# A newly written order for attention and a mixer on one core: other loads wait, and small tiles stand in 58 stretches for 52

## The chip, the core and the metric

The kernel runs on one core of a Trainium2 chip. The metric is the device time of one execution in microseconds (us); the time before is the median of three runs. The engines are TensorE (PE in the profile; its weight loads are PEld), VectorE (DVE), ScalarE (ACT), GpSimd (POOL) and SyncE (SP). Loads from memory are issued by GpSimd; stores and transposing transfers by SyncE.

## What is computed

Eight batches of 12 heads, 448 tokens, head size 64, then a mixer over tokens and channels on the 768 joined columns:

```python
scores = scale * np.matmul(q, k.transpose(0, 1, 3, 2))
attn = np.maximum(scores, 0.0) ** 2 / S
x = np.matmul(attn, v)                      # heads side by side: (8, 448, 768)
h = np.maximum(xt @ w_tok1, 0.0) @ w_tok2   # xt: x with tokens last; 448 -> 256 -> 448
u = x + h.transpose(0, 2, 1)
h2 = np.maximum(u @ w_ch1, 0.0) @ w_ch2     # 768 -> 1536 -> 768
out = u + h2
```

The inputs are float32, the products are made in bfloat16.

## The kernel before

The attention is done in 24 groups of four heads, three groups to a batch. The program first makes a list of named operations with what each depends on, and then emits them in the order of a table, `ORDER` (line 73), a text of some two thousand words. A word is a name, and behind the colon the PSUM banks of a product (`S0.4:75`), the engine of an evacuation (`:A` ScalarE, `:D` VectorE), or the gate of a load. Each engine takes its own words in the order of the table, so the table fixes five queues and, by their place, what waits behind what. `Order.run` (line 51) reads it. The names that matter here:

- `ldk9.0`, `ldq..`, `ldv..`: loads of half a group's keys, queries or values, cast on the way (line 371, GpSimd). `ldf` brings the first queries through SyncE and ScalarE, and `cast` turns them to bfloat16. `wt`, `wc1.i` and `wc2.i` load the weights of the two mixers (lines 382, 389, 397, 406); `wc1.i` covers four of the twelve column blocks `e` of the first channel product, and the second product needs all three `wc2.i`.
- `ident` makes the identity matrix on GpSimd. `T s` transposes keys and queries of groups 0 to 9 on TensorE against it (line 472), `cp` copies the result out of PSUM. From group 10 on `ik`/`iq` rearrange them and `xk`/`xq` transpose them by a transfer of SyncE's queue (line 497).
- `S s.c`: one block of scores, four products of 64 x 64 tiles (line 515), a quartet; `r` takes the positive part out of PSUM, `q` squares it, `V s.c` multiplies by the values (line 542, also a quartet), `xe` evacuates.
- `xd s` transposes the group's result by a transfer of SyncE's queue (line 566; for groups 0 to 5 TensorE does it, `X`, line 579, with the copy `xc`), `t1` and `t2` are the token mixer (lines 588 and 597) with `rt` between, `u` adds (line 601), `ub` transposes u by a transfer (line 610).
- `C1` (line 623) or, from batch 2 on, `M1` with its sums `tu`, `s1`, `d1`, `y1` (line 780) is the first channel product; `C2` (line 713) and `M2` with `h`, `d2` (line 847) the second. `M1` and `M2` make seven products of eight by sums of blocks, `w1` and `w2` are such sums of the weights. `st` stores 64 rows of the result (line 668).
- `fill:b*n` puts products without use on TensorE (line 967): n quarters of a product of 512 columns, whole ones first and the rest of 128.

A gate makes a load wait on GpSimd's queue until the named transfer of SyncE has landed:

```python
            if o.eng == 'POOL' and how:
                self.behind(o.ins, self.ops[how].ins)
```

Every load also waits for the one eight places before it, and SyncE's transfers do the same among themselves, since each of the two queues has eight semaphores; all loads land in the order of their issue. On TensorE a product of 64 x 64 tiles (`T`, `S`, `V`) and one of 128 rows (all others) follow each other in stretches of a kind; the table before has 52 stretches of small tiles.

## Time and profile before

| what | value |
|---|---|
| median of three runs | 344.29 us (342.73 to 345.22) |
| the profiled execution | 346.45 us, span 344.4 us |
| granted TensorE clock | 1.000 |
| TensorE, VectorE, ScalarE, GpSimd busy | 97%, 86%, 73%, 27% of the span |
| longest wait of TensorE | 3.1 us, once |
| read from memory and written | 43.38 MB and 11.01 MB |

A row of the timeline has start and length in us, engine, line, operation, what is written from what is read, and in brackets the engine's idle time before it with what ended it. Lengths of TensorE's rows overlap, since products are pipelined: what a block takes is read from its start to the start of the next. A row by stretches has, behind the window, its length and then the busy us of PE, PEld, DVE, ACT and POOL with their counts, the clock, the share of the transfer engines and GB/s. A row of waits has the sum, the count and the longest. A row of transfers has the count, the size and the median time from issue to landing.

### The profile page before, as it was taken

How to read it: one execution, taken by the hardware profiler on the slowest of the kernel's cores; microseconds unless marked ns; L12 is line 12 of the kernel's file. 1: busy time of each engine (PE TensorE's matmuls, PEld its weight loads, DVE VectorE, ACT ScalarE, POOL GpSimd, SP SyncE). 2: the span in 40 equal slices, each digit the busy share in tenths (PEclk: the TensorE clock that was granted, in tenths of full speed). 3: DMA queues.
4: the chain of work that ended last, by engine and by line, in shares of the span. 5: the costliest groups of instructions: out<-in, count | busy, mean ns of one | idle time of the engine just before them, and what ended most of it. 6: DMA issues, size and time to landing. Idle time of an engine off the chain costs nothing.

```text
span 344.4 us, 9413 instructions
## 1 busy us (share of the span) xinstructions
PE 333.3 (97%) x3796; PEld 222.5 (65%) x3797; DVE 295.0 (86%) x571; ACT 250.0 (73%) x462; POOL 92.3 (27%) x157
## 2 busy tenths in 40 slices
PE   7899999999999999699999999999999999999995
PEld 3456555655565658575678556876578777887763
DVE  2999998899899999699999999888986986838783
ACT  3999999858899799689999888979875832221000
POOL 9994322725160341323240712020020000000000
PEclk9999999999999999999999999999999999999999
DMA  8999999989999999999999998796676113432255
GB/s 147 191 183 199 206 209 169 135 136 157 190 184 153 174 150 101 186 233 141 195 178 199 164 162 155 137 162 122 140 151 90 23 32 72 94 82 62 69 148 152
DMA packets 98940, 50.20 MB, mean 146 GB/s; under 512 B 71568, under 2 KB 95952, under 8 KB 98896
## 3 DMA queue, kind: packets, MB, share of 16 engines
q0 software_dynamic: 25136, 21.47, 46.3%
q1 hardware_dynamic: 72736, 26.92, 44.7%
q10 hardware_dynamic: 1024, 1.21, 1.2%
q8 instruction: 29, 0.48, 0.5%
q14 instruction: 15, 0.12, 0.1%
HBM read 43.38 MB, written 11.01 MB: 158 GB/s over the span
## 4 chain that ended last, share of the span: by engine, by line
PE 86%; DMA 6%; POOL 3%; DVE 2%; ACT 1%; issue 0%; POOLq 0%; ACTq 0%; DVEq 0%
PE m_ps L847 24%; PE m_ps L780 18%; PE sc_ps L515 10%; PE acc_ps L542 8%; PE m_ps L623 8%; PE t_ps L588 6%; PE h_ps L597 5%; PE m_ps L713 5%; DMA x_sb<-xT 4%; POOL arena L371 2%; DMA arena<-in_k_dram 2%; PE kqT_ps L472 1%; DMA arena<-in_q_dram 1%; PE x_ps L579 1%; DVE arena L796 1%; DVE uT L601 1%
## 5 line engine op out<-in xcount | busy, mean ns | idle before, releaser
L343 ACT ACTIVATE arena<-sc_ps 128x448 bf16<-128x448 f32 x232 | 117.1, 594 | 15.9 <-PE sc_ps L515 15.4
L355 ACT ACTIVATE arena<-arena 128x896 bf16<-128x896 bf16 x76 | 72.4, 970 | 0.6 <-DVE arena L345 0.3
L345 DVE TENSOR_SCALAR arena<-sc_ps 128x448 bf16<-128x448 f32 x104 | 62.1, 616 | 3.9 <-PE sc_ps L515 3.5
L357 DVE TENSOR_TENSOR arena<-arena 128x896 bf16<-128x896 bf16 x92 | 55.1, 615 | 1.1 <-ACT arena L343 0.6
L515 PE MATMUL sc_ps<-arena 64*64 64x448 bf16 x672 | 54.2, 357 | 1.5 <-ACT arena L349 1.2
L371 POOL DMA_DIRECT2D arena<-in_q_dram x46 | 28.6, 624 | 80.6 <-DMA arena<-arena 28.0
L371 POOL DMA_DIRECT2D arena<-in_v_dram x48 | 29.7, 620 | 55.4 <-DMA out_dram<-out_sb 19.5
L780 PEld LDWEIGHTS <-wc 128*128 128x128 bf16 x432 | 40.9, 98 | 5.2 <-issue 2.3
L542 PE MATMUL acc_ps<-arena 64*64 64x448 bf16 x672 | 42.7, 350 | 0.2
L371 POOL DMA_DIRECT2D arena<-in_k_dram x48 | 29.9, 630 | 26.4 <-DMA out_dram<-out_sb 10.7
L515 PEld LDWEIGHTS <-arena 64*64 64x64 bf16 x672 | 22.0, 105 | 22.5 <-issue 13.8
L780 PEld LDWEIGHTS <-ws 128*128 128x128 bf16 x324 | 30.8, 98 | 4.0 <-issue 1.8
L847 PE MATMUL m_ps<-wc,r 128*128 128x384 bf16 x162 | 30.3, 327 | 0.0
L601 DVE TENSOR_TENSOR uT<-h_ps,xT 128x448 bf16<-128x448 f32 x48 | 29.1, 616 | 1.2 <-PE h_ps L597 0.9
L623 PE MATMUL m_ps<-uT,wc 128*128 128x448 bf16 x144 | 29.9, 353 | 0.0
L847 PEld LDWEIGHTS <-r 128*128 128x128 bf16 x216 | 20.4, 98 | 14.8 <-issue 2.5
L542 PEld LDWEIGHTS <-arena 64*64 64x64 bf16 x672 | 20.9, 106 | 11.3 <-issue 3.1
L588 PE MATMUL t_ps<-x_sb,wt 128*128 128x256 bf16 (+1 forms) x216 | 25.0, 261 | 3.1 <-DMA x_sb<-xT 3.1
L796 DVE CUSTOM_DVE_ANT_0 r<-r,m_ps 128x448 bf16<-128x448 f32 x32 | 19.6, 616 | 8.8 <-PE m_ps L780 3.7
L793 ACT ACTIVATE arena<-m_ps 128x448 f32<-128x448 f32 x18 | 9.3, 542 | 23.7 <-PE m_ps L780 8.3
L780 PE MATMUL m_ps<-uT,wc 128*128 128x224 bf16 x216 | 25.4, 259 | 0.0
L597 PE MATMUL h_ps<-wt,r_sb 128*128 128x448 bf16 x96 | 25.1, 353 | 0.0
(86 smaller groups left out, 508.5 us busy)
## 6 DMA issues: line engine op xcount, KB each, us to landing
out_dram<-out_sb SPq DMA_DIRECT2D x42, 192.0 KB, 3.3
arena<-in_k_dram POOLq DMA_DIRECT2D x48, 112.0 KB, 5.0
arena<-in_v_dram POOLq DMA_DIRECT2D x48, 112.0 KB, 5.3
arena<-in_q_dram POOLq DMA_DIRECT2D x46, 112.0 KB, 4.9
wc<-in_moe_w_ch_dram POOLq DMA_DIRECT2D x6, 768.0 KB, 13.2
out_dram<-arena SPq DMA_DIRECT2D x4, 192.0 KB, 2.6
out_dram<-out_sb SPq DMA_DIRECT2D x8, 96.0 KB, 2.1
out_dram<-out_sb ACTq DMA_DIRECT2D x8, 96.0 KB, 2.4
```

What stands on the lines that cost most here:

```text
L343: nc.scalar.activation(out, ps, AF.Relu)
L345: nc.vector.tensor_scalar(out=out, in0=ps, scalar1=0.0, scalar2=None, op0=ALU.max)
L355: nc.scalar.activation(x, x, AF.Square)
L357: nc.vector.tensor_tensor(out=x, in0=x, in1=x, op=ALU.mult)
L371: o.ins = nc.gpsimd.dma_start(out=raws[t][s % NR][64 * half:64 * (half + 1)], in_=src[b, h0:h0 + 2].rearrange('e (p c) d -> p e (c d)', c=KC))
L515: nc.tensor.matmul(o.ps[e][64 * half:64 * (half + 1), :S], lhsT=lhsT, rhs=rhs, start=True, stop=True, skip_group_check=True)
L542: nc.tensor.matmul(o.ps[half][64 * e:64 * (e + 1), :S], lhsT=r[rows, e, c * D:(c + 1) * D], rhs=sq[rows, e, :], start=c == 0, stop=c == KC ...
L588: nc.tensor.matmul(o.ps[:, j, :], lhsT=wt1[:, c, j * 128:(j + 1) * 128], rhs=x_sb[:, p0:p1, c, :], start=c == 0, stop=c == 3)
L597: nc.tensor.matmul(o.ps[:, :S], lhsT=r1[:, j, a * 128:(a + 1) * 128], rhs=wt2[:, j, :], start=j == 0, stop=j == JC - 1)
L623: nc.tensor.matmul(ps[:, :S], lhsT=wc1[:, g, e * 128:(e + 1) * 128], rhs=uT[:, g, off:off + S], start=g == 0, stop=g == CC - 1)
L780: nc.tensor.matmul(o.ps[:, j * HB:(j + 1) * HB], lhsT=lhs[:, g, (e + j) * 128:(e + j + 1) * 128], rhs=rhs[:, g], start=j == g == 0 and not ...
L847: nc.tensor.matmul(o.ps[:, :HN], lhsT=lhs[:, e], rhs=rhs[:, e], start=e == 0 and not on, stop=e == EC // 2 - 1, skip_group_check=True)
```

## The change

The table `ORDER` is replaced by another; the rest of the program, the operations and what each depends on are the same. In the new table

- small tiles stand in 58 stretches, not 52;
- 84 loads have a gate, not 57, and the gates are other transfers;
- four fills of 30 quarters in all (`5*6`, `4*4`, `0*6` ahead of the first transposes, `0*14` a little later) become one of seven (`3*7`);
- some evacuations change engine: ScalarE has 80 squares for 76 and 230 evacuations of scores for 232, VectorE 13 copies `cp` for 10 and 9 `rt` for 6;
- all queues are ordered otherwise. The first and two later rows of the table, before and now:

```diff
-fill:5*6 ldf.0 fill:4*4 fill:0*6 ident ldf.1 ldk0.1 ldk0.0 ldq2.1 ldq1.1 ldq1.0 ldk1.0 cast1.0:D cast1.1:A
+cast0.1:D T0.1:0 cp0.1:A T0.0:1 cp0.0:D S0.4:23 ldq2.1 ldv0.1 ldk2.0 S0.6:45 ldv0.0 r0.4.0:D r0.4.1:A S0.2:67
+fill:3*7 S1.2:62 r1.0.1:A q0.6:D r0.3.1:D S1.3:01 T2.0:34 q0.0:D ldv1.1 r1.2.0:A q0.2:A q0.5:D ldk4.0 S1.1:57
...
-wc2.0 t2.2.1:4 r3.5.0:A u2.0:D C1.0.2a:2 r3.5.1:A q3.0:D r3.6.1:A S4.4:76 q3.5:D r4.2.0:A V3.0:50 V3.1
+q3.2:D r3.3.0:A t1.2.1:0 q3.5:D cp4.1:D rt2.0:A ldv4.0:ub0.2 C1.0.2a:5 rt2.1:A t2.2.1:6 q3.1:A wc1.1 wc2.1
```

In the lists below, taken from the built programs, `DMASWn` is a wait for the load eight places before, `DMAHWn` one for a transfer of SyncE's queue, which is the gate, and `PE`, `DVE`, `Activation` one for an engine that still reads the buffer.

GpSimd at the program's start, behind its constants, before:

```order
L999 UNCONDITIONAL_BRANCH [waits barrier_Pool_Activation_PE_DVE_SP_gather]
masks.py:197 MEMSET ident 128x128
masks.py:199 ISA
masks.py:199 AFFINE_SELECT ident<-ident 128x128 [waits Pool_49]
L371 DMA arena<-in_k_dram 64x2x448 x2
L371 DMA arena<-in_q_dram 64x2x448 x3
L371 DMA arena<-in_k_dram 64x2x448 x2
```

and now (the new table has one line more, so that line numbers behind it are one higher):

```order
L1000 UNCONDITIONAL_BRANCH [waits barrier_Pool_Activation_PE_DVE_SP_gather]
L372 DMA arena<-in_k_dram 64x2x448 x2
L372 DMA arena<-in_q_dram 64x2x448
L372 DMA arena<-in_k_dram 64x2x448 x2
L372 DMA arena<-in_q_dram 64x2x448
masks.py:197 MEMSET ident 128x128
masks.py:199 ISA
masks.py:199 AFFINE_SELECT ident<-ident 128x128 [waits Pool_49]
```

The identity has moved behind six loads, and the first two key loads to the front.

GpSimd among the weight loads (wc1.1, then wc2.0, wc2.1 and wc2.2), before:

```order
L397 DMA wc_67<-in_moe_w_ch_dram 128x6x512 [waits DMASW1_49]
L371 DMA arena<-in_k_dram 64x2x448 [waits DMASW2_49,PE_49]
L406 DMA wc_68<-in_moe_w_ch_dram 128x4x768 [waits DMASW3_49]
L371 DMA arena<-in_q_dram 64x2x448 [waits DMASW4_49,PE_49]
L406 DMA wc_68<-in_moe_w_ch_dram 128x4x768 [waits DMASW5_49]
L371 DMA arena<-in_v_dram 64x2x448 [waits DMASW6_49,PE_49]
L406 DMA wc_68<-in_moe_w_ch_dram 128x4x768 [waits DMASW7_49]
```

and now, from ldv4.0 behind ub0.2 (DMAHW2) through wc1.1 and wc2.1, ldq7.0 behind ub0.4 (DMAHW3), to wc2.2 and wc2.0:

```order
L372 DMA arena<-in_v_dram 64x2x448 [waits DMAHW2_49,DMASW0_49]
L398 DMA wc_67<-in_moe_w_ch_dram 128x6x512 [waits DMASW1_49]
L407 DMA wc_68<-in_moe_w_ch_dram 128x4x768 [waits DMASW2_49]
L372 DMA arena<-in_q_dram 64x2x448 [waits DMAHW3_49,DMASW3_49,PE_49]
L372 DMA arena<-in_k_dram 64x2x448 [waits DMASW4_49]
L372 DMA arena<-in_v_dram 64x2x448 [waits DMASW5_49,PE_49]
L372 DMA arena<-in_k_dram 64x2x448 [waits DMASW6_49]
L372 DMA arena<-in_v_dram 64x2x448 [waits DMASW7_49,PE_49]
L372 DMA arena<-in_q_dram 64x2x448 [waits DMASW0_49]
L407 DMA wc_68<-in_moe_w_ch_dram 128x4x768 [waits DMASW1_49]
L407 DMA wc_68<-in_moe_w_ch_dram 128x4x768 [waits DMASW2_49]
```

Two transfers of u, which before came behind all weights, now stand ahead of some of them, and GpSimd's queue stops for each.

GpSimd around xd10, before, from ldq16.1 behind xk13 to ldv12.0:

```order
L371 DMA arena<-in_q_dram 64x2x448 [waits DMAHW0_49,DMASW7_49,DVE_49]
L371 DMA arena<-in_v_dram 64x2x448 [waits DMASW0_49,PE_49]
L371 DMA arena<-in_k_dram 64x2x448 [waits DMASW1_49,Activation_49]
L371 DMA arena<-in_v_dram 64x2x448 [waits DMAHW1_49,DMASW2_49]
L371 DMA arena<-in_k_dram 64x2x448 [waits DMASW3_49,DVE_49]
L371 DMA arena<-in_v_dram 64x2x448 [waits DMASW4_49]
L371 DMA arena<-in_q_dram 64x2x448 [waits DMASW5_49,DVE_49]
L371 DMA arena<-in_v_dram 64x2x448 [waits DMASW6_49]
```

and now, from ldq15.1 behind ub2.1 to ldv12.1, with ldk14.0 behind xd10 itself (the sixth row):

```order
L372 DMA arena<-in_q_dram 64x2x448 [waits DMAHW6_49,DMASW1_49]
L372 DMA arena<-in_q_dram 64x2x448 [waits DMAHW5_49,DMASW2_49]
L372 DMA arena<-in_q_dram 64x2x448 [waits DMAHW2_49,DMASW3_49]
L372 DMA arena<-in_k_dram 64x2x448 [waits DMAHW4_49,DMASW4_49,Activation_49]
L372 DMA arena<-in_v_dram 64x2x448 [waits DMAHW3_49,DMASW5_49,PE_49]
L372 DMA arena<-in_k_dram 64x2x448 [waits DMAHW5_49,DMASW6_49]
L372 DMA arena<-in_q_dram 64x2x448 [waits DMAHW1_49,DMASW7_49]
L372 DMA arena<-in_v_dram 64x2x448 [waits DMASW0_49]
```

Of eight loads two had a gate; now seven have one.

## The prediction

> **What bounds the kernel now.** I read the page's shares first, then the busy time by stretches, then TensorE's waits, then the chain that ended last.

> ```profile
> span 344.4 us, 9413 instructions
> PE 333.3 (97%) x3796; PEld 222.5 (65%) x3797; DVE 295.0 (86%) x571; ACT 250.0 (73%) x462; POOL 92.3 (27%) x157
> ...
> 8.00:30.00 22.00, 20.26 (x408) 11.75 (x410) 21.25 (x42) 21.45 (x48) 18.64 (x31) 1.00 1.24 188
> 120.00:142.00 22.00, 18.93 (x217) 13.24 (x215) 18.77 (x39) 17.65 (x36) 7.74 (x13) 1.00 1.36 139
> 142.00:260.00 118.00, 118.00 (x1268) 82.01 (x1266) 109.27 (x211) 104.63 (x190) 25.71 (x43) 1.00 1.06 163
> ```

> TensorE is busy for 97%, and from 142 to 260 us without a hole: there the time is the sum of its own products. Two stretches are different. From 8 to 30 us VectorE (21.25 of 22) and ScalarE (21.45) are full and TensorE waits for banks that they empty, inside what counts as busy:

> ```profile
> 17.09 2.13 PE L515 MATMUL sc_ps<-arena 64*64 64x448 bf16 x16
> 19.27 0.22 PE L472 MATMUL kqT_ps<-ident,arena 64*64 64x64 bf16 x2
> ...
> 105.50 0.36 PE L542 MATMUL acc_ps<-arena 64*64 64x448 bf16 x4
> 105.69 0.36 PE L515 MATMUL sc_ps<-arena 64*64 64x448 bf16 x4
> 105.87 0.55 PE L542 MATMUL acc_ps<-arena 64*64 64x448 bf16 x8
> 106.36 1.15 PE L847 MATMUL m_ps<-wc,r 128*128 128x384 bf16 x6
> 107.43 0.76 PE L515 MATMUL sc_ps<-arena 64*64 64x448 bf16 x12
> 108.13 1.15 PE L847 MATMUL m_ps<-wc,r 128*128 128x384 bf16 x6
> 109.11 1.14 PE L847 MATMUL m_ps<-ws,sums 128*128 128x384 bf16 x6
> ```

> Four score blocks took 2.18 us from start to start at 17 us, 0.55 each; later one takes 0.19 (105.50 to 105.69). The other stretch is 120 to 142 us, with 18.93 of 22 busy:

> ```profile
> PE t_ps L588 <- DMA x_sb<-xT: 3.1, 1, 3.1
> ...
> 128.53 12.31 DMA x_sb<-xT
> ```

> One transposing transfer (xd10) takes 12.31 us and t1.10 stands still for 3.1 us. That is the only long wait.

> **Price of a stretch of small tiles.** The same rows give it. Two quartets and the change to 128-row tiles take 0.49 us (105.87 to 106.36), 0.11 more than 2 x 0.19. The large block before a stretch takes 1.07 (106.36 to 107.43) where one followed by a large block takes 0.98 (108.13 to 109.11): 0.09. Three quartets that are a whole stretch take 0.70 (107.43 to 108.13), 0.13 over 3 x 0.19, which is the 0.11 and 0.02 at the entry; and the first large block behind a stretch gives 0.01. Together about 0.23 us. The written order now has 58 stretches for 52, so 6 x 0.23 = **+1.4 us**, and TensorE has no cover for it, since from 50 us it is the bound. I take 1.2 to 1.6.

> **The start.** The rows are those of the first transposes, of the loads and copies ahead of them, and of the pace of the two engines behind them.

> ```profile
> 1.19 4.02 PE L414 MATMUL warm_ps<-out_sb 128*128 128x512 bf16 x9 [1.19 <-DVE out_sb L411]
> 5.01 1.66 PE L970 MATMUL fill_ps<-out_sb 128*128 128x512 bf16 x7
> 6.60 0.97 PE L472 MATMUL kqT_ps<-ident,arena 64*64 64x64 bf16 x56
> 8.24 2.06 PE L515 MATMUL sc_ps<-arena 64*64 64x448 bf16 x24 [0.67 <-ACT arena L349]
> ...
> 0.74 0.20 POOL masks.py:197 MEMSET ident<- 128x128 bf16 x1 [0.29 <-POOLq L988]
> 1.44 1.32 POOL L371 DMA_DIRECT2D arena<-in_k_dram  x2
> ...
> 7.27 0.92 ACT L349 ACTIVATE arena<-kqT_ps 128x896 bf16<-128x896 bf16 x1 [1.76 <-PE kqT_ps L472]
> 7.62 0.62 DVE L351 COPY arena<-kqT_ps 128x896 bf16<-128x896 bf16 x1 [2.28 <-PE kqT_ps L472]
> 8.71 2.22 DVE L345 TENSOR_SCALAR arena<-sc_ps 128x448 bf16<-128x448 f32 x4 [0.47 <-PE sc_ps L515]
> ```

> Now the first transposes stand behind the fills until 6.60, both halves go at once, and the first score starts at 8.24, when the second copy is done. In the changed order the fills are gone, the first two key loads go out ahead of the identity matrix, 0.7 us earlier (1.44 to 0.74), and each half's copy starts when its half is there. GpSimd makes the identity behind six loads (1.32 for two by the row), at some 4.5 to 5.1 us, so half 1 can go at about 5.2 and half 0 at 5.9, when the third cast is done; its copy of 0.62 then ends near 7.1. The two engines get their first scores 1.0 us earlier, some 0.2 of a possible 1.2 left to slower transposes.

> Whether TensorE keeps that is set by the queue behind. VectorE has 62 operations of the order ahead of the end of the fourth group (V3.6) where it had 59, ScalarE 63 for 66; the two pace at 0.53 us (VectorE) and 0.43:

> ```profile
> 18.01 1.68 DVE L357 TENSOR_TENSOR arena<-arena 128x896 bf16<-128x896 bf16 x3
> 19.61 0.61 DVE L345 TENSOR_SCALAR arena<-sc_ps 128x448 bf16<-128x448 f32 x1
> ...
> 18.05 3.35 ACT L343 ACTIVATE arena<-sc_ps 128x448 bf16<-128x448 f32 x7
> 21.04 0.85 ACT L349 ACTIVATE x_sb<-x_ps 128x512 bf16<-128x512 bf16 x1
> ```

> Two to three VectorE operations more eat 1.0 to 1.5 us of the lead there. ScalarE, which was as late as VectorE, comes out ahead and has ten operations fewer by the end of the sixth group (101 for 111), so the waits between 30 and 60 us shrink. I take **-0.6 us**, between -1.3 (all of the earlier start and some waits) and +0.5 (the extra VectorE work decides).

> **Late transfers.** xd10 was issued amid a burst of loads:

> ```profile
> 124.36 0.60 POOL L371 DMA_DIRECT2D arena<-in_q_dram  x1 [9.32 <-DVE sums L688]
> 127.28 0.65 POOL L371 DMA_DIRECT2D arena<-in_v_dram  x1
> 129.42 0.60 POOL L371 DMA_DIRECT2D arena<-in_q_dram  x1 [1.49 <-DVE arena L351]
> ...
> u_sb<-uT SPq DMA_TRANSPOSE x36, 4.8
> arena<-arena SPq DMA_TRANSPOSE x28, 4.6
> x_sb<-xT SPq DMA_TRANSPOSE x18, 5.4
> wc<-in_moe_w_ch_dram POOLq DMA_DIRECT2D x6, 768.0 KB, 13.2
> ```

> Six loads went out back to back from 124.36 and two more from 129.42; against them xd10 took 12.31 us, where the median is 5.4. TensorE had 8.6 us of products between xd10 and t1.10, counted by the block prices; now it has 8.2. So the distance does not cure it. What may is that 84 loads wait for a transfer of SyncE's queue where 57 did, and around xd10 the loads stand behind ub2.1, ub2.0, xk13, ub2.2 and xd10 itself. Against the usual 5.4 us, 8.2 is enough. New tight places are xk12 and xd9, 5.4 and 5.2 us ahead of their use, where the medians are 4.6 and 5.4, but no load is written for some 7 us around them. I take the 3.1 us as gone and **+0.8** for new late ones: -2.3 in this execution, between -3.1 and 0.

> **The end.** The last product is followed by one sum and two stores, as before; I cost it at nothing either way.

> ```profile
> 339.04 1.14 PE L847 MATMUL m_ps<-wc,arena 128*128 128x384 bf16 x6
> 340.22 0.55 DVE L862 TENSOR_TENSOR out_sb<-out_sb,m_ps 128x384 f32<-128x384 f32 x1 [0.55 <-PE m_ps L847]
> ```

> The other moved sums and evacuations lie under TensorE's full stretch (VectorE 109.27, ScalarE 104.63 of 118 us); without that cover two sums would cost about 1 us.

> **Sum.** +1.4 - 0.6 - 2.3 = -1.5. The profiled execution took 346.45 us (span 344.4), 2.16 over the median of 344.29 of the three others. Either these were without most of the 3.1 us wait; then only 0.9 of it is left to win, and the sum is 344.29 + 1.4 - 0.6 - 0.9 + 0.8 = 345.0. Or the profile adds 2.16 throughout, and it is 344.29 - 1.5 = 342.8. I cannot tell them apart and forecast the middle, **343.9 us**.

> **Rivals.** (1) The weights come late; this one ends slower. GpSimd's queue now stops twice among the weight loads, at ldv4.0 for ub0.2 and at ldq7.0 for ub0.4, where it had no such stop; SyncE's first u transfer waited 55.4 us for the weights instead. Behind the second stop stand wc2.2 and wc2.0, and the first second-stage product needs both; that product now starts at 63.85:

> ```profile
> 63.85 1.08 PE m_ps L847 x6
> ...
> SPq L610 <- DMA wc<-in_moe_w_ch_dram: 55.4, 1, 55.4
> ```

> It has 47.0 us of products ahead of it by the block prices, so 16.8 us were start and waits; u2.0 has 21.5 ahead of it in the changed order and is ready near 38 us, the first second-stage product has 48.0 and comes near 64. If ub0.4 takes its 4.8 us or some more, the six small loads between go out at 44 to 47, the two weights at about 48, and with 13.2 us to landing they are there near 61. From about 50 us on, each microsecond that ub0.4 lands later is one that TensorE waits; at 54 that is 4 us, 344.3 + 4 = 348.3. For it speaks that ub0.2 and ub0.4 run against weight loads, against it that such a transfer is alone in its queue. (2) The gates do not help: some other transfer is as late as xd10 was, and 3.1 us stays. Then 344.29 + 1.4 - 0.6 + (0 to 2.2), about 346. (3) TensorE starts at half speed and stays there. The nine warm products of 512 columns take 0.42 us each (1.19 to 5.01), 0.83 ns a column, where the blocks of 384 take 0.16 (0.98 for six), 0.43 ns. The fills kept it busy until its rate had doubled. Up to the end of the third group it has 47 quartets (8.9 us) and, as an estimate, 5 us of transposes and token products in 22 us; at half rate 14 are 28, so about +6 if it lasts so long, 349.5, and under 0.5 if the rate doubles in the first 5 us, as the two emptying engines are slower than that anyway. [...] (4) All goes well: no late transfer, the whole earlier start, and half of the small waits after 30 us gone: 344.29 - 3.1 - 1.3 + 1.4 - 0.8 = 340.5.

> **How the numbers follow.** Forecast 0.50 (342 to 345.5), (1) 0.12, (2) 0.20, (3) 0.05, (4) 0.13. A measurement here tells about 1% from no change, so 340.9 and 347.7 are the bounds. (4) gives 0.11 faster and the forecast's edge 0.01; (1), (3) but a part and the upper end of (2) give 0.15 slower; 0.73 is left for the same. The range is 341.0 to 347.6: it takes in the bounds of the start and of the late transfers, and leaves out (1) and (3) at full price and half of (4).

> **What would show it.** Right: a score block first at about 7.1 us; no TensorE wait for x_sb over 1 us; a stretch of small tiles still 0.23 us and 58 of them; loads pausing behind transposing transfers. Wrong: a wait before the first product with wc2 near 64 us; quartets at 0.38 us beyond 15 us; xk12 or xd9 in TensorE's list of waits; any hole over 1 us between 142 and 260 us.

## The result: slower by about 1%, and the profile after

The changed kernel took 349.2 us in the median of eight runs (346.65 to 353.64), the kernel before 344.75 us beside it (342.73 to 350.14). The ratio is 1.012, with a 95% interval of 1.007 to 1.017: slower by 1.2%, or 4.2 us, where 343.9 us and no change were forecast. The two slowest runs of each kernel, which were in a slower state, are left out of the ratio, though not of the medians.

The page's first lines:

```profile
span 347.3 us, 9403 instructions
PE 336.3 (97%) x3789; PEld 221.4 (64%) x3789; DVE 296.6 (85%) x575; ACT 249.9 (72%) x458; POOL 92.2 (27%) x157
```

The busy time by stretches, in the columns of before:

```profile
8.00:30.00 22.00, 19.70 (x382) 11.35 (x386) 21.26 (x43) 20.58 (x44) 15.86 (x27) 1.00 1.17 168
120.00:142.00 22.00, 21.94 (x238) 15.17 (x236) 21.04 (x42) 20.03 (x41) 8.31 (x14) 1.00 1.28 181
142.00:260.00 118.00, 116.75 (x1233) 79.41 (x1231) 107.11 (x208) 101.41 (x186) 28.62 (x48) 1.00 1.10 163
```

The profiled execution took 349.09 us, with a span 2.9 us longer than before (347.3 for 344.4). The hole of 120 to 142 us is closed (21.94 of 22 us busy for 18.93), as predicted. In its place stand many small ones: from 142 to 260 us TensorE now lacks 1.25 of 118 us where it lacked nothing. TensorE's waits behind its warm products, longest first:

```profile
PE x_ps L580 <- ACT xT L553: 0.9, 1, 0.9
PE sc_ps L516 <- DMA arena<-arena: 0.8, 1, 0.8
...
PE t_ps L589 <- DMA x_sb<-xT: 0.3, 1, 0.3
```

None is over 0.9 us, and the wait for x_sb is down from 3.1 to 0.3. The start, on TensorE's timeline:

```profile
5.72 2.01 PE L473 MATMUL kqT_ps<-ident,arena 64*64 64x64 bf16 x56 [0.51 <-POOL ident masks.py:199]
8.46 1.33 PE L516 MATMUL sc_ps<-arena 64*64 64x448 bf16 x12 [0.73 <-DVE arena L352]
9.58 0.96 PE L473 MATMUL kqT_ps<-ident,arena 64*64 64x64 bf16 x56
```

The transposes go 0.9 us earlier than before but take 2.01 us for 0.97, so that the first score comes at 8.46 us, not at the predicted 7.1 (before 8.24). Its three blocks take 1.12 us to the next transposes (8.46 to 9.58), 0.37 each and twice the 0.19 of later: TensorE is at half rate. The trace's record of the granted clock opens at 13.79 us; in the run before it opened at 6.28.

To compare executions I use the time that TensorE has lost: the moment at which the product behind a group's last value product starts (V9.6 is the last one of the tenth group), less the sum of all products up to there by the block prices and 0.23 us for a stretch. Each further column has what was lost since the column before it. The runs that the account below rests on:

| order and run | lost up to V9.6 | to V10.6 | to V12.6 | to V17.6 | to V23.6 | clock opens |
|---|---|---|---|---|---|---|
| before | 16.7 | 0.1 | 3.4 | 0.2 | 0.3 | 6.3 |
| before, fewer fills | 16.1 | 0.1 | 0.2 | 5.4 | 0.3 | 5.5, half 8.9 to 12.3 |
| before, no fills | 17.5 | 0.1 | 0.2 | 0.2 | 0.3 | 16.6 |
| before, 14 stretches more | 17.3 | 1.0 | 0.7 | 0.9 | 0.3 | 5.7 |
| before, fewer fills, eight gates more | 17.0 | 0.1 | 0.2 | 2.0 | 5.5 | 3.9, half 7.4 to 14.2 |
| changed | 17.4 | 1.6 | 0.2 | 2.2 | 1.3 | 13.8 |
| changed, opening fills | 16.8 | 1.4 | 2.9 | 2.3 | 0.8 | 5.8 |
| changed, one fill | 16.8 | 1.9 | 0.2 | 1.2 | 2.1 | 6.6 |
| changed, no gates | 16.3 | 2.7 | 8.0 | 5.3 | 6.5 | 5.7 |
| changed, fill and key transfer | 17.1 | 0.3 | 0.2 | 1.3 | 1.8 | 4.5, half 7.9 to 11.3 |
| changed, key transfer | 17.8 | 0.4 | 0.2 | 1.1 | 0.8 | 5.0 |
| changed, fill, key transfer and two places more | 16.5 | 0.3 | 0.2 | 2.5 | 0.8 | 5.3 |

The last column tells of the start alone. Later the clock was at half in four of these runs: at 183.0 to 186.4 us with fewer fills, 145.7 to 149.1 with all opening fills, 138.9 to 145.7 and 210.5 to 214.0 without gates, and 212.2 to 215.6 with eight gates more. The profiled execution with fewer fills was the slowest of its twelve (347.6 us), and its 5.4 us before V17.6 are an accident of its own.

### The profile page after: what moved, and what is told of

The parts are those of the page before. It is cut to its first block, busy times and chain, and to the rows that moved or that the text cites. A ratio compares the mean times of both kernels' runs of the same rounds, so it can differ in the third digit from the quotient of the medians.

```text
span 347.3 us, 9403 instructions
## 1 busy us (share of the span) xinstructions
PE 336.3 (97%) x3789; PEld 221.4 (64%) x3789; DVE 296.6 (85%) x575; ACT 249.9 (72%) x458; POOL 92.2 (27%) x157
## 4 chain that ended last, share of the span: by engine, by line
PE 75%; DMA 14%; DVE 3%; issue 2%; ACT 2%; POOL 2%; SPq 1%; POOLq 0%; DVEq 0%; ACTq 0%
PE m_ps L781 18%; PE m_ps L848 17%; PE sc_ps L516 9%; PE m_ps L624 8%; PE acc_ps L543 8%; PE t_ps L589 5%; PE h_ps L598 4%; PE m_ps L714 4%; DMA arena<-in_k_dram 4%; DMA out_dram<-out_sb 3%; DMA arena<-in_v_dram 2%; POOL arena L372 2%; DMA x_sb<-xT 2%; PE kqT_ps L473 1%; DMA arena<-in_q_dram 1%
## 5 line engine op out<-in xcount | busy, mean ns | idle before, releaser
L344 ACT ACTIVATE arena<-sc_ps 128x448 bf16<-128x448 f32 x230 | 113.6, 562 | 14.8 <-PE sc_ps L516 12.4
L356 ACT ACTIVATE arena<-arena 128x896 bf16<-128x896 bf16 x80 | 74.9, 965 | 0.3
L346 DVE TENSOR_SCALAR arena<-sc_ps 128x448 bf16<-128x448 f32 x106 | 62.9, 616 | 6.8 <-PE sc_ps L516 5.6
L516 PE MATMUL sc_ps<-arena 64*64 64x448 bf16 x672 | 57.6, 368 | 1.7 <-DMA arena<-arena 0.8
L358 DVE TENSOR_TENSOR arena<-arena 128x896 bf16<-128x896 bf16 x88 | 53.0, 616 | 0.9
L543 PE MATMUL acc_ps<-arena 64*64 64x448 bf16 x672 | 45.1, 351 | 0.9 <-ACT arena L344 0.7
L516 PEld LDWEIGHTS <-arena 64*64 64x64 bf16 x672 | 22.4, 107 | 24.2 <-issue 15.4
L543 PEld LDWEIGHTS <-arena 64*64 64x64 bf16 x672 | 22.1, 106 | 11.5 <-issue 4.3
L848 PEld LDWEIGHTS <-sums 128*128 128x128 bf16 x180 | 16.9, 98 | 12.9 <-issue 1.4
## 6 DMA issues: line engine op xcount, KB each, us to landing
wc<-in_moe_w_ch_dram POOLq DMA_DIRECT2D x6, 768.0 KB, 10.1
```

The source lines that it names most:

```text
L344: nc.scalar.activation(out, ps, AF.Relu)
L346: nc.vector.tensor_scalar(out=out, in0=ps, scalar1=0.0, scalar2=None, op0=ALU.max)
L356: nc.scalar.activation(x, x, AF.Square)
L358: nc.vector.tensor_tensor(out=x, in0=x, in1=x, op=ALU.mult)
L516: nc.tensor.matmul(o.ps[e][64 * half:64 * (half + 1), :S], lhsT=lhsT, rhs=rhs, start=True, stop=True, skip_group_check=True)
L543: nc.tensor.matmul(o.ps[half][64 * e:64 * (e + 1), :S], lhsT=r[rows, e, c * D:(c + 1) * D], rhs=sq[rows, e, :], start=c == 0, stop=c == KC ...
```

## The experiments

The theories: (A) the start without fills leaves TensorE at half rate for longer; (B) six more stretches of small tiles cost 1.4 us; (C) gates make loads and transfers late (or keep them from being late); (D) one transfer of keys is too late in every execution of the new order.

### The start: fills put back, and fills taken away

```diff
-cast0.1:D T0.1:0 cp0.1:A
+cast0.1:D fill:5*6 fill:4*4 fill:0*6 T0.1:0 cp0.1:A
```

> The changed kernel with the three opening fills of the kernel before (5*6, 4*4, 0*6) put back ahead of its first transposes; nothing else differs. In the profile of the changed kernel TensorE's clock record opens at 13.79 us, before at 6.28. Theory A, the cold start costs the time: the clock opens near 6.3 us again, score blocks behind it take 0.19 to 0.44 us and not 0.37 throughout, TensorE's end comes 1 to 2.5 us earlier and the time is near 347.2 (0.995 of the changed kernel's 348.8). Theory B, the time went to the 58 stretches and to late transfers behind 100 us: the fills only push the first transposes from 5.7 to 6.6 us, the clock opens early but the time stays at 348.5 to 349.5.

```diff
-cast0.1:D T0.1:0 cp0.1:A
+cast0.1:D fill:0*6 T0.1:0 cp0.1:A
```

> The changed kernel with one fill of six quarters (0*6, one product of 512 columns and two of 128, 0.53 us at half rate) ahead of its first transposes, which covers just the 0.5 us in which TensorE waits for the identity matrix. Theory A (cold start): if that gap of 0.5 us is what keeps the clock shut, it opens near 6.3 us as in the kernel before, and the time falls to about 347 or a little below, better than with all three fills since the transposes are not pushed back; if the gaps behind it (0.24 us among the first transposes, 0.7 before the first score) keep it shut too, the clock still opens behind 10 us and the time stays at 348.8. Theory B (stretches and late transfers): no change of the time, 348.5 to 349.5, whenever the clock opens.

In the kernel before, the other way round:

```diff
-fill:5*6 ldf.0 fill:4*4 fill:0*6 ident ldf.1
+ldf.0 ident ldf.1
...
-fill:0*14
+fill:0*7
```

> The kernel before with its three opening fills left out and the later one cut from 14 quarters to 7, as many as the changed kernel has; its order is otherwise its own. Theory A (cold start): the clock opens behind 10 us and the time rises by 1 to 3 us to 346 to 347.5, ratio 1.003 to 1.009, although 2.3 us of fills are gone from TensorE. Theory B (stretches and late transfers): the fills only stood in the way, the first transposes start at about 5.3 us and not 6.6, and the time is the same or up to 1.3 us less, 343.4 to 344.7.

and with `fill:0*7` left out as well:

> The kernel before with all its fills left out, the nine warm products staying. If fills at the start only stand in the way and the clock opens whenever a window of 3.4 us happens to be full of products: the time is that of the kernel with fewer fills or up to 0.5 us less, ratio 0.995 to 0.998. Theory A (cold start): without the last fill the clock stays shut behind 14 us in most executions and the time rises by 1 us or more, ratio 1.000 to 1.004.

Measured: all three fills 350.22 us, ratio 1.012 (1.007 to 1.018); one fill 347.14 us, 1.006 (1.002 to 1.010); before with fewer fills 344.11 us, 0.997 (0.993 to 1.000); before with none 344.11 us, 1.000 (0.997 to 1.004). The clock opened where theory A says in the first two (5.8 and 6.6 us), and in the last not before 16.6; with fewer fills it opened at 5.5, where theory A has it behind 10. And the time does not follow it. By the table's first column a late clock costs 0.8 to 1.4 us up to V9.6 (17.5 for 16.1 or 16.7 in the order before, 17.4 for 16.3 in the changed one). And it is a draw: the changed order without gates (below) has the same start, and there it opened at 5.74 us, its score blocks taking 0.20 us (three in 0.59):

```profile
7.73 0.76 PE L516 MATMUL sc_ps<-arena 64*64 64x448 bf16 x12 [0.71 <-DVE arena L352]
8.32 0.68 PE L473 MATMUL kqT_ps<-ident,arena 64*64 64x64 bf16 x56
```

So theory A holds for about 1 us in some executions, and not for 4. Why all three fills end 3 us behind one fill stays open; 1 us of it could be seen, in the accident that the profile of the first shows. TensorE and GpSimd there:

```profile
144.78 1.95 PE L543 MATMUL acc_ps<-arena 64*64 64x448 bf16 x28 [2.10 <-DMA arena<-in_v_dram]
...
147.03 1.30 PE L781 MATMUL m_ps<-sums,ws 128*128 128x224 bf16 x6
148.13 1.24 PE L781 MATMUL m_ps<-sums,wc 128*128 128x224 bf16 x6
149.20 0.74 PE L781 MATMUL m_ps<-uT,ws 128*128 128x224 bf16 x6
...
140.41 0.60 POOL L372 DMA_DIRECT2D arena<-in_v_dram  x1 [6.03 <-DMA out_dram<-out_sb]
```

and the stretch behind it, where the granted clock stands third from the end:

```profile
145.70:149.10 3.40, 3.40 (x32) 2.07 (x21) 1.87 (x4) 1.81 (x3) 0.00 (x0) 0.50 1.50 181
```

A load of values (ldv12.0) stood 6.03 us at its gate, the store st5.64, and TensorE waited 2.1 us for it. For the next 3.4 us the clock was at half: blocks that take 0.58 us took 1.1 (147.03 to 148.13 to 149.20), 1 us more.

### The gates

All 86 taken out of the changed kernel, those of 84 half-group loads and of two weight loads (`ldv4.0:ub0.2` becomes `ldv4.0`, and so on):

> The changed kernel with all 86 gates of its loads taken out, so that a load waits only for its buffer and for the load eight places before. Theory C1, the gates are what makes loads and transfers late (GpSimd's queue stands at a gate, xk11 and the waits of TensorE at 109, 112, 161, 172, 190 us follow): these waits of 3.5 us in all go, and the time falls by 2 to 3 us to about 346.3. Theory C2, the gates keep loads out of the way of transposing transfers, as meant: without them some transfer takes 10 us or more, TensorE gets a wait for x_sb or for transposed keys of over 1 us, and the time rises by 1 to 4 us to 350 to 353. Neither: within 0.7 us of 348.8.

Measured: 363.5 us in the median of six runs, 357.1 to 367.9. TensorE's two costliest waits are for transfers, whose medians hide it (4.9 us for 5.3 with gates): of the transposing transfers of keys, queries and x whose landing the trace shows, ten of 42 took over 8 us, xd10 13.3, where in the changed kernel it was one of 46 (and seven of 40 in the kernel before, with 57 gates):

```profile
PE sc_ps L516 <- DMA arena<-arena: 5.4, 4, 2.6
PE t_ps L589 <- DMA x_sb<-xT: 4.1, 3, 1.5
PE m_ps L781 <- DVE uT L689: 2.7, 1, 2.7
```

C2 holds, and by far more than expected: the gates are worth some 14 us by the medians, and 10 by the fastest run of each kernel (357.1 for 346.65). That more of them would be worth more does not follow. Eight words of the order before, with fewer fills:

```diff
-ldk15.0 ldk17.0 ldq19.0 ldq20.1 ldk20.1 ldv18.0 ldq20.0 ldv18.1
+ldk15.0:xd9 ldk17.0:xq13 ldq19.0:xd10 ldq20.1:xk15 ldk20.1:xq17 ldv18.0:xd14 ldq20.0:xq19 ldv18.1:ub4.2
```

> The kernel before with its fills cut (no opening fills, 7 quarters) and eight gates more (65 for 57), each on a transfer of SyncE that was under way when the load went out: ldk15.0 behind xd9, ldk17.0 behind xq13, ldq19.0 behind xd10, ldq20.1 behind xk15, ldk20.1 behind xq17, ldv18.0 behind xd14, ldq20.0 behind xq19, ldv18.1 behind ub4.2. If more gates are what makes late transfers rarer (the changed kernel has 86 gates, and its longest transposing transfer took 9.4 us where the kernel before shows 12.3): no transposing transfer over 9 us, no TensorE wait over 1 us between 120 and 200 us, and a time 0.5 to 1 us under the kernel with fewer fills (ratio 0.992 to 0.995). Rival: GpSimd's queue stands at these gates and the loads behind them come late in their turn: ratio 0.998 or more, with new waits of TensorE.

Measured: 354.8 us, ratio 1.025 (1.019 to 1.031). The profiled execution was the fastest of the six (350.25 us), so it shows only a part of this. GpSimd's loads in one place without these gates (the run without fills, whose lines are numbered one lower), the first and the last of twelve, with pauses of under 0.7 us between:

```profile
187.72 0.59 POOL L370 DMA_DIRECT2D arena<-in_q_dram  x1 [14.01 <-ACT arena L354]
...
196.69 0.60 POOL L370 DMA_DIRECT2D arena<-in_q_dram  x1
```

and with them, with SyncE's issue of xd17 and xd16 in the last row:

```profile
194.80 0.59 POOL L371 DMA_DIRECT2D arena<-in_q_dram  x1 [3.39 <-DMA arena<-arena]
197.07 0.59 POOL L371 DMA_DIRECT2D arena<-in_v_dram  x1 [1.68 <-DMA u_sb<-uT]
...
201.72 0.68 POOL L371 DMA_DIRECT2D arena<-in_q_dram  x1
...
198.91 3.45 SPq L566 DMA_TRANSPOSE x_sb<-xT  x2
```

TensorE's longest wait there:

```profile
PE t_ps L588 <- DMA x_sb<-xT: 4.9, 2, 3.5
```

GpSimd stood 3.39 us for xq19 and 1.68 for ub4.2, and what had waited behind went out as one burst from 197.07 to 202.4 us, against xd17 and xd16, which were issued in the middle of it. Without the gates the loads were out at 197.3, ahead of both. xd16 took 10.8 us (6.2 without), TensorE waited 3.5, and the clock went to half for 212.2 to 215.6 us. A gate does not take a load away; it moves it, and what stands behind it, onto the next transfer.

### The late key transfer

In four profiles of the changed order TensorE loses 1.4 to 2.7 us between V9.6 and V10.6 (in the fourth, without gates, 1.45 of the 2.7 is a wait for x). SyncE's queue, then GpSimd's loads, then TensorE, in the changed kernel:

```profile
101.03 1.24 SPq L669 DMA_DIRECT2D out_dram<-out_sb  x2
102.31 1.79 SPq L611 DMA_TRANSPOSE u_sb<-uT  x1
104.15 0.59 SPq L669 DMA_DIRECT2D out_dram<-out_sb  x1
104.83 1.29 SPq L498 DMA_TRANSPOSE arena<-arena  x1
106.24 1.47 SPq L567 DMA_TRANSPOSE x_sb<-xT  x1
...
105.23 0.59 POOL L372 DMA_DIRECT2D arena<-in_k_dram  x1 [7.25 <-DMA out_dram<-out_sb]
105.81 0.60 POOL L372 DMA_DIRECT2D arena<-in_v_dram  x1
...
108.38 2.12 PE L848 MATMUL m_ps<-wc,r 128*128 128x384 bf16 x12
111.33 0.76 PE L516 MATMUL sc_ps<-arena 64*64 64x448 bf16 x12 [0.82 <-DMA arena<-arena]
```

The row of 104.83 is xk11. SyncE's queue is issuing without a pause, three stores and a transfer of u ahead of it, and xk11 lands at 111.28, just ahead of the row of 111.33, S11.0, which waited 0.82 us. Right behind xk11 two loads go out: ldk12.1, which had stood 7.25 us at its gate, the store st0.64, and ldv11.0. The place of xk11 and of the rearrangement ik11 alone was changed:

```diff
-st0.64 ... r9.3.1:D ... st1.64 ... iq12:D C1.1.11:3 ik11:D ub1.3 st1.0 ... xk11
+st0.64 ... ik11:D r9.3.1:D ... xk11 st1.64 ... iq12:D C1.1.11:3 ub1.3 st1.0
```

> The changed kernel with one fill of six quarters ahead of its first transposes, and with the rearranging of the eleventh group's keys (ik11) and their transfer (xk11) written earlier: ik11 ahead of r9.3.1 on VectorE, xk11 ahead of the store st1.64 on SyncE, which had st1.64, ub1.3 and st1.0 ahead of it. In the profile of the changed kernel and of both kernels made from it with other starts TensorE loses 1.3 to 1.9 us between the products of the tenth and of the eleventh group (V9.6 to V10.6), where the kernel before loses 0.1; xk11 goes out at 103 to 105 us and lands 6.5 to 8.3 us later, when S11.0 has been waiting for 0.9 to 1.7 us. Theory D, SyncE's queue brings that transfer too late in every execution: xk11 goes out some 3 us earlier, the wait is under 0.3 us, and the time falls by 1.2 to 1.6 us against the kernel with the fill alone, to 345.7, ratio to the kernel before near 1.002. Rival E, late transfers come by chance and the next tight one takes the place (t1.8.0 behind xd8, or S12 behind xk12): the wait moves to the next place within 15 us, and the time stays near 347.1, ratio 1.006.

> The changed kernel with nothing altered but the earlier place of ik11 and xk11 (ik11 ahead of r9.3.1, xk11 ahead of st1.64); its start is the changed kernel's own, without an opening fill. Theory D (that one transfer is late in every execution and costs 1.5 us): the loss between V9.6 and V10.6 falls from 1.6 to 0.3 us, and the ratio to the kernel before from 1.0122 to 1.008. Rival: with the start as it is, another place takes the wait and the ratio stays at 1.010 to 1.014. It also draws the start once more: if the clock that opened at 13.8 us is the rule without a fill, it opens behind 10 us here too and TensorE's time without products up to V9.6 is 17.2 to 17.5 us; if that was chance, the clock opens near 5.7 us as in the run without gates, with 16.1 to 16.4 us.

Measured: with the fill 346.56 us, ratio 1.005 (1.002 to 1.009); alone 346.76 us, 1.007 (1.004 to 1.010). In the second the row is

```profile
101.57 1.30 SPq L498 DMA_TRANSPOSE arena<-arena  x1
...
108.60 2.12 PE L848 MATMUL m_ps<-wc,r 128*128 128x384 bf16 x12
110.65 1.01 PE L516 MATMUL sc_ps<-arena 64*64 64x448 bf16 x12
```

and S11.0 does not wait. The loss there falls to 0.4 us, and the ratio from 1.012 to 1.007 (1.9 us; the intervals overlap, so the size rests on the trace, 1.2 to 1.6). Theory D holds for this wait; rival E in part: with the fill the gain over the fill alone is 0.1% where 0.4% was expected.

What the move shows is that the place costs this much, not why the transfer was slow there. In the three profiles where xk11 took 6.5 to 8.3 us, the two loads went out within 1 us of it. In the three where it stood earlier, the loads came 2.7 to 3.4 us behind it, and it took 3.0 to 3.6. Without gates it kept its place, with xd8 and xq12 behind it as before, but no load went out until 2.6 us behind it, and it took 4.3 us (S11.0 waited 0.8 us there too, since xk11 was issued later against the products). So the gate at st0.64, which puts two loads beside xk11, is as likely a cause as SyncE's queue; no run moved that gate alone.

On top of the fill and the earlier transfer two more places were eased: `ldv12.0:st5.64` to `ldv12.0`, and t2.12.1 put behind t1.13.0.

> The kernel with the opening fill and the earlier key transfer, and two more tight places of the changed order eased: ldv12.0 has no gate any more (it stood behind the store st5.64; in the run with all opening fills GpSimd stood there for 6.0 us, the values landed at 144.7 us and V12.0 waited 2.1 us, and the clock was at half for the window behind it), and t2.12.1, which waits 0.3 to 0.6 us for a bank behind M1.3.0.6 in every profile of this order, stands behind t1.13.0. If these are what is left of the changed order's own waits, the wait at M1.3.0.6 is under 0.1 us, V12.0 does not wait, and the ratio to the kernel before falls from 1.0053 to 1.002 to 1.004, of which the six stretches (1.4 us, 0.004) are the whole. Rival: the load let go at ldv12.0 joins the burst behind it and makes xd11 or xk14 late: ratio 1.005 to 1.008, with a wait of over 1 us between 130 and 150 us.

Measured: 346.83 us, ratio 1.007 (1.004 to 1.010): nothing gained. V12.0 and t2.12.1 no longer wait, but waits came out elsewhere, for sums at 160 us and for keys at 170 (S16). The ratio is the rival's; its wait between 130 and 150 us is not there:

```profile
PE m_ps L848 <- DVE sums L689: 0.9, 1, 0.9
...
PE sc_ps L516 <- DMA arena<-arena: 0.6, 1, 0.6
```

### The stretches

14 more in the kernel before, each as in this place:

```diff
-S16.1:43 ... M1.3.0.7 ...
+M1.3.0.7 S16.1:43 ...
```

> The kernel before with 14 stretches of small tiles more (66 for 52) between 95 and 200 us: in 14 places the last score block of a stretch is written behind the first product of 128 rows that followed it; nothing is left out or added. Price theory (0.23 us for a stretch): the time rises by 14 x 0.23 = 3.3 us, ratio 1.0095 (1.007 to 1.012), and TensorE's sum without waits from 318.7 to 322.0 us. Rival, that stretches are nearly free since a change of tiling hides in the pipeline and the 0.23 us was the wait for something else: ratio 0.998 to 1.003.

Measured: 349.8 us, ratio 1.015 (1.011 to 1.020), 5.3 us where 3.3 were expected. A single block is a stretch of its own here:

```profile
174.46 0.73 PE L780 MATMUL m_ps<-sums,wc 128*128 128x224 bf16 x6 [0.16 <-ACT r L793]
175.13 0.38 PE L515 MATMUL sc_ps<-arena 64*64 64x448 bf16 x4
175.44 0.75 PE L780 MATMUL m_ps<-uT,ws 128*128 128x224 bf16 x6
176.03 1.04 PE L588 MATMUL t_ps<-x_sb,wt 128*128 128x256 bf16 x8
```

It takes 0.31 us (175.13 to 175.44) for 0.19, and the product ahead of it 0.67 for the 0.59 of the next: 0.20 us of the 0.23. The other 2 us are waits: from V9.6 to V17.6 the table has 2.6 us lost for 0.5 in the old order without an accident (no fills), since what was put between has to wait for its banks and sums.

Seven fewer, in the changed order (with the fill and the earlier transfer) and in the order before (with fewer fills). One of the seven in each:

```diff
-M2.1.4.5:5 ... M2.1.4.6 ... S15.1:72 ... S15.4:36 S14.5:10
+S15.1:72 ... S15.4:36 S14.5:10 M2.1.4.5:5 ... M2.1.4.6
...
-M2.0.3.2:3 ... S10.5:56 ... S11.0:72 S11.3:14 ... M2.0.3.1:0 ... M2.0.3.5:3 ... S10.6:65 ... S10.2:14 S11.1:27
+S10.5:56 S11.0:72 S11.3:14 ... S10.6:65 ... S10.2:14 S11.1:27 M2.0.3.2:3 ... M2.0.3.1:0 ... M2.0.3.5:3
```

> The kernel with the fill and the earlier key transfer, and in addition seven stretches of small tiles fewer (51 for 58): single products or pairs between two stretches (X0.1, C1.0.10, C1.1.9, C1.1.5, M1.3.4.4, M2.1.4.5 with M2.1.4.6, M1.5.2.5 with M1.5.0.1) stand behind the second stretch, so that the two become one; nothing is left out. Price theory (0.23 us for a stretch): TensorE's sum of products and changes falls from 320.15 to 318.5 us, and the time by 1.6 us, ratio to the kernel before lower by 0.005 than without the merging (0.997 where that is 1.002). Rival: what a change of tiling costs is hidden by other waits, or the products that come later by 0.2 to 0.9 us make their readers wait: no difference between the two kernels, within 0.002.

> The kernel before with its fills cut as in the earlier run (no opening fills, 7 quarters for 14), and with seven stretches of small tiles fewer (45 for 52): t1.0.1, t1.2.1 with t1.2.0, M2.0.3.2, then M2.0.3.2 to M2.0.3.5, M2.0.5.7 with t1.9.0 and t2.8.1, M2.1.4.1, and M2.1.0.7 with M2.1.2.7 stand behind the small stretch that followed them. Price theory: 7 x 0.23 = 1.6 us less than the kernel with the fewer fills alone (ratio to the kernel before 0.9966), so a ratio of 0.992 and some 342.3 us, faster than both kernels. Rival: the products that now come later by 0.2 to 0.6 us make u, the transfers behind it and the evacuations later by as much, and these waits eat the gain: ratio 0.995 to 0.999.

Both came out far slower: 353.96 us, ratio 1.027 (1.022 to 1.033), and 352.37 us, 1.022 (1.017 to 1.028). The second, where six score blocks now follow each other:

```profile
108.21 1.87 PE L515 MATMUL sc_ps<-arena 64*64 64x448 bf16 x12
110.39 1.73 PE L515 MATMUL sc_ps<-arena 64*64 64x448 bf16 x9 [0.31 <-ACT arena L343]
113.14 0.59 PE L515 MATMUL sc_ps<-arena 64*64 64x448 bf16 x3 [1.02 <-ACT arena L343]
113.66 1.78 PE L847 MATMUL m_ps<-wc,r 128*128 128x384 bf16 x5
```

Six blocks take 5.4 us (108.21 to 113.66), 0.9 each, where in the kernel before three took 0.70 (107.43 to 108.13, in the prediction) and two large products stood ahead of the next three: the two engines empty banks more slowly than TensorE fills them here (1.02 and 0.31 us of waits for ScalarE stand in brackets), and the large product between was their time. The last 0.9 us ran at half clock, which fell at 112.7 us amid these waits. The first shows the same: at 160 us three blocks take 2.05 us (160.78 to 162.83) with 0.64 of waiting ahead of them.

```profile
160.78 2.12 PE L516 MATMUL sc_ps<-arena 64*64 64x448 bf16 x12 [0.64 <-ACT arena L344]
162.83 1.48 PE L848 MATMUL m_ps<-ws,sums 128*128 128x384 bf16 x8
```

So the price theory is right for what a change of tiling costs and wrong as advice: neither of these two mergings got the stretches back.

## Why the prediction was wrong, step by step

**Price of a stretch: right.** With 0.23 us each, the sum of products and changes is 318.7 us before and 320.1 now, and the parts of the trace that wait for nothing fit it with 58 and with 66 stretches.

**The start: wrong in this execution.** -0.6 was taken (bounds -1.3 and +0.5) and +0.7 came (17.4 for 16.7), outside the bounds. The bound was made without the clock. Rival 3 saw it, at under 0.5 us if the rate doubled in the first 5 us and +6 if it stayed to 30; it stayed to 13.8 and cost about 1.1, by the run of the same start whose clock opened at 5.7 (16.3). Where the clock opened early and stayed open, the changed order lost 16.3 to 16.8 us in four of five runs, three of them with a fill (16.7 before): from 0.4 of the predicted gain to none of it. In the fifth x came late for t1.7, among other waits, and it was 17.8.

**Late transfers: the step that failed.** "I take the 3.1 us as gone and +0.8 for new late ones: -2.3". In the profile the wait did go: xd10 lands in 4.18 us, not 12.31. But the gain was not there to be had in the median. Three other profiles of the old order with its queues of loads and transfers untouched (fewer fills, no fills, more stretches) lose 0.2 to 0.7 us between V10.6 and V12.6, where the profiled run lost 3.4; xd10 took 7.7, 5.9 and 3.1 us there. The wait was an accident of one execution in four; the prediction's own first reading ("these were without most of the 3.1 us wait", 345.0) was the better one, though it still counted 0.9 us of it as a gain, and the middle of two readings was not a forecast. And the new late one was about twice its price of 0.8 and regular: xk11 and what waits behind it, 1.4 to 1.9 us in the changed kernel and its two other starts. The prediction set the distance to the use, in products, against the medians (xk12 5.4 us, xd9 5.2) and listed what looked tightest; xk11 was not among it: by the block prices it had some 6 us of products ahead of its use, where the old order gave it 15.9, and against the median of 4.6 that looked enough. What it left out is SyncE's queue ahead of xk11 and the two loads that the gate at st0.64 lets go beside it. From its issue to landing 6.5 to 8.3 us passed; how much of that is the loads, the runs do not part. The gates that were to keep loads off the transfers put two of them on this one.

**Small waits: not in the sum.** From V12.6 to V23.6 the changed order loses 3.5 us in the profile, the old one 0.5. Three of the places, in the changed kernel:

```profile
162.47 1.15 PE L848 MATMUL m_ps<-wc,sums 128*128 128x384 bf16 x6 [0.42 <-DVE sums L689]
...
173.54 0.54 PE L598 MATMUL h_ps<-wt,r_sb 128*128 128x448 bf16 x2 [0.20 <-ACT arena L344]
...
190.86 0.73 PE L781 MATMUL m_ps<-sums,wc 128*128 128x224 bf16 x6 [0.44 <-ACT r L794]
```

The prediction costed the moved sums and evacuations at nothing because VectorE had 109 of 118 us of work. That is cover for their sum, not for the order in which they come. The one at 173 us (t2.12.1) is in every profile that has it in this place, 0.3 to 0.6 us from start to start.

**The end: right,** 4.2 us behind the last product in both.

**The rivals.** (1) No product waits for the weights for over 0.5 us in any of the profiles, so the two stops at ub0.2 and ub0.4 cost little or nothing. (2) Gates do help, by 14 us against none; but its result, that some other transfer is late, is nearest to what happened. (3) is answered above; its 349.5 follows from none of the sums (343.9 + 6 is 349.9). (4) did not occur.

**The account.** Of 4.2 us: 1.4 for the stretches; 1.2 to 1.9 for xk11, by the traces and the ratio when it was moved (beside the fill the ratio moved by only 0.1%, under 0.3 us); the remaining 0.9 to 1.6 is put down to the late clock in some executions and the small waits, which the runs do not part. In the profile the lost wait of 3.1 us hid it: +1.4, +0.7 at the start, +1.5 for xk11, +3.0 behind V12.6, less 3.2 for xd10 and 0.6 between V23.6 and the last product, is but for rounding the 2.9 us by which the span grew. Of what it named beforehand, no wait for x_sb over 1 us, no hole over 1 us from 142 to 260 us and neither xk12 nor xd9 among the waits came true; the first score at 7.1 us did not. None of the twelve kernels is faster than the kernel before beyond its interval; the nearest is that kernel with fewer fills, 0.997 (0.993 to 1.000). That one fill, one transfer and two places together stay at 1.007, where the stretches alone would give 1.004, is left open.

## What to carry to other kernels

A long wait in one profiled execution is a draw until a second execution shows it, above all when that execution was slower than the others by about as much: price it by how often it occurs. When an order is written anew, walk along the queue of each transfer (what is issued ahead of it, what shares its time), not only along the products between it and its use. Gates and changes between kinds of products look like pure costs in the sum; before one is moved or taken out, ask which engine used that time. For a gate ask also which transfer is under way when it opens.

## What the runs showed of the hardware

**The same transfer took from 3 to 13 us.** xd10, always the same bytes: 4.2 us in the changed kernel, 3.1, 5.9, 7.7 and 12.3 in four executions of the order before, 13.3 without gates. From 5 us before its issue to 2 us behind it, three and four loads went out beside the 4.2 and the 3.1 us, five to eight beside the others; that the loads are the cause is likely by this and by xk11, but no run moved loads alone.
